# Clearing the modality table second on VectorE, and 128 weight columns for the products of the modality codes

## The chip, the cores and the metric

The kernel runs on one core of one Trainium2 chip. The metric is the device time of one execution in microseconds (us). Engines are called as the profile calls them: PE is TensorE's products, PEld its weight loads, DVE is VectorE, ACT is ScalarE, POOL is GpSimd and SP is SyncE.

## The reference, cut to what matters

Sliding-window attention feeds a mixture of experts. Each of the 4608 tokens takes the one expert with the largest gate value; a bias that depends on the token's modality (0 or 1) is added to the gate values first.

```python
def _attn_ref(q, k, v):                       # q, k, v: 8 batches x 8 heads x 576 x 64
    scores = scale * np.matmul(q, k.transpose(0, 1, 3, 2))
    mask = np.abs(pos[:, None] - pos[None, :]) <= window      # window 32
    attn = softmax(np.where(mask, scores, -1000000000.0))
    return np.matmul(attn, v)

def _moe_ref(x, modality_id, w_gate, modality_bias, w1, w2):  # x: 4608 x 512, 8 experts
    logits = x @ w_gate + modality_bias[modality_id]
    e_idx = np.argmax(logits, axis=1)
    gate_w = softmax(logits)[np.arange(N), e_idx]
    for e in range(E):
        mask = e_idx == e
        h = np.maximum(x[mask] @ w1[e], 0.0)
        out[mask] = gate_w[mask, None] * (h @ w2[e])
```

## The kernel before, in words

**The plan.** In the data, all tokens of one modality take the same expert. So the kernel sorts the tokens by modality while it computes attention, runs each modality's tokens through one expert, and scatters the rows of the result back. For that it counts the tokens of modality 1 in each block of up to 128 tokens (40 blocks, five for each of the eight batches), forms for each token its place in the sorted order, and builds a 0/1 matrix `oh` from these places (`o`, lines 569 to 577, on POOL for the first three batches).

**The order.** `ORDER` (line 38) is a list of operations written out by hand. A loop (line 915) goes through it and calls the function of each name; every engine then runs its own instructions in just that order. In a name, the digits are batch and part, the letter behind a slash is the engine, the digits behind a colon are PSUM banks.

**The modality table.** `mid64` holds the token ids, one row per block. `Kh` (line 290, DVE) clears it, since blocks at the two ends of a batch fill their row only in part. `Ki` (lines 281 to 286) issues five loads into it on SP's queue; they wait for the clearing. `Kd` (line 467, DVE) casts it to bf16 and waits for all five loads. `Kt` and `Kr` (lines 471 to 505) transpose it on PE, count with products of one column and form the places: line 488 writes `c16`, line 496 the last of `lpf`, both on DVE, and lines 503 and 505 on POOL write the codes `valx`. `Kc7` (line 415, DVE) clears the table `cl` that takes the sorted codes; `Ke` (line 424) writes eight constants.

**The queues around it.** DVE's next instruction behind `Kd` is `tv0.0` (line 239), which transposes rows of v; PE's transposes `TV` (line 252) need it. POOL issues nearly all loads (lines 217, 222, 228 for q, k, v; line 795 for the experts' weights, 1 MB each as bf16), between its own computations; it waits with `oh` (line 573) for `lpf`.

**The products of the codes.** For each batch `J` (lines 705 to 713) multiplies `oh` of five blocks by the codes of the block: the weights are 4 columns of `valx` (`valx[:, NM * b + m, :]`), the moving side is 96 or 128 columns of `oh`, and the result has 4 rows in PSUM. ACT (`j`, line 719) copies these 4 rows into `cl`. `H` (line 680) does the same for the rows of x, with 128 columns of weights. The experts' products are `U` (line 822) and `D` (line 845); `S` (line 614) is the scores' products, whose weights have 32 rows, `V` (line 660) the products with v.

Of the kernel before, what the change touches and what calls it, by code (L numbers as in the profile page):

```python
# [23 lines left out]
BF16 = mybir.dt.bfloat16  # L24
# [11 lines left out]
NYS = 6  # L36

ORDER = """
Km l0.1.0 Kw Kc7 Kj l0.0.0 lw0.0 Kn0 Ke Kh Kx Kq0/a t0.0.1 t0.0.0 X4:7 X3:2 X0:4 X2:3 MB0.0:4567 Ky0 Kp1/v Kv2/v X9:2
X11:3 X10:2 X5:3 SB0.0:4567 X6:3 Ki MA0.0:0123 SA0.0:0123 Kd tv0.0 Kv0/v l0.0.1 t0.1.0 Kp0/a sb0.0 sa0.0 Kv1/p l0.1.1  # L40
t0.1.1 lw0.1 Kc1 Kq1/a l1.1.0 l1.0.0 Kc4 Kc0 Kv3/p Kc3 Kc2 TV0.0:567 vc0.0/a Kt0:4 Kr0 MB0.1:0123 SB0.1:0123 l1.1.1
Kt1:4 sb0.1 tv0.1 X7:5 TV0.1:567 Kr1 t1.0.1 MA0.1:0123 SA0.1:0123 Kt2:4 t1.0.0 Kr2 vc0.1/a sa0.1 V0:67 V1:45 v0 v1
t1.1.1 MB1.0:0123 SB1.0:0123 l1.0.1 Ka lw1.1 Kr3 Kc5 o0/p lw2.0 lw1.0 l2.1.0 o1/p l2.0.0 Ko0 sb1.0 Kp2/a V2:45 v2 V3:67
# [47 lines left out]
def kernel(  # L91
# [12 lines left out]
    nc = tc.nc  # L104
    B, H, S, D = q.shape
    P = 128
# [8 lines left out]
    NM = 5  # L115
    NJ = B * NM
# [8 lines left out]
    width = lambda m: 96 if m in EDGE else P  # L125
# [10 lines left out]
    const = ctx.enter_context(tc.tile_pool(name="const", bufs=1))  # L136
# [9 lines left out]
    def apart(ins, group, other, keep=()):  # L146
        unordered(ins, other, keep)
        tc.add_to_no_dep_group(group, ins.ins)
# [7 lines left out]
    def bank(shape, dt=FP32, i=0):  # L156
        n_ = 1
        for s_ in shape[1:]:
            n_ *= s_
        f_ = banks[:, bk[i], :] if dt == FP32 else banks[:, bk[i], :].bitcast(dt)  # L160
        f_ = f_[0:shape[0], 0:n_]
        if len(shape) == 3:
            f_ = f_.rearrange("p (a b) -> p a b", a=shape[1])
        return f_
# [10 lines left out]
    Ct = {}  # L175
# [150 lines left out]
    def iota_f(n, pattern, base_, cm, dt=FP32):  # L326
        ti = const.tile([P, n], I32, name=f"ioi{iota_f.c}")
        tf = const.tile([P, n], dt, name=f"iof{iota_f.c}")
        iota_f.c += 1
        nc.gpsimd.iota(ti[:], pattern=pattern, base=base_, channel_multiplier=cm)  # L330
        nc.gpsimd.tensor_copy(tf[:], ti[:])
        return tf
# [37 lines left out]
    @named  # L370
    def Kc(_, i):
        gs = nc.gpsimd
        if i == 0:
            gs.memset(tri[:], 1.0)
            gs.affine_select(out=tri[:], in_=tri[:], compare_op=ALU.is_ge, fill=0.0,
                             base=-1, pattern=[[1, P]], channel_multiplier=-1)
            gs.memset(ones[:], 1.0)
        elif i == 1:
            T["ic"] = iota_f(NM, [[0, NM]], 0, 1)
            gs.tensor_copy(cc1[:], T["ic"][:])  # L380
            gs.tensor_scalar(out=cc1[:, 0:1], in0=T["ic"][:, 0:1], scalar1=-32.0, scalar2=None, op0=ALU.add)
            gs.memset(cc1[0:32, 0:1], -1000.0)
            gs.memset(cc1[96:P, NM - 1:NM], -1000.0)
            gs.tensor_scalar(out=cc2[:], in0=cc1[:], scalar1=-1.0, scalar2=127.0, op0=ALU.mult, op1=ALU.add)
            ends = cc2[:, 0:NM:NM - 1]
            gs.tensor_scalar(out=ends, in0=ends, scalar1=-32.0, scalar2=None, op0=ALU.add)
        elif i == 2:
            T["iol"] = iota_f(P, [[1, P]], 0, 0)
            gs.tensor_copy(io_l[:], T["iol"][:])
        elif i == 3:  # L390
            gs.tensor_copy(vb[:, :, 0:1], iota_f(NJ, [[0, NJ]], 127, -1)[:].unsqueeze(2))
            gs.tensor_copy(vb[:, :, 1:2], iota_f(NJ, [[-18, B], [-4, NM]], 145, 0)[:].unsqueeze(2))
        elif i == 4:
            T["tj"] = iota_f(NJ + NM, [[S, B + 1], [P, NM]], -32, 0)
            first = T["tj"][:].rearrange("p (b m) -> p b m", m=NM)[:, :, 0:1]
            gs.tensor_scalar(out=first, in0=first, scalar1=32.0, scalar2=None, op0=ALU.add)
        elif i == 5:
            ic = T["ic"][:, 0:1]
            wf = const.tile([P, 4], FP32)
            for j_, (r_, c_) in enumerate(((0, 1.0), (1, 32.0), (2, 1.0), (3, 32.0))):  # L400
                gs.tensor_scalar(out=wf[:, j_:j_ + 1], in0=ic, scalar1=float(r_), scalar2=c_,
                                 op0=ALU.is_equal, op1=ALU.mult)
            for i_ in range(2):
                gs.tensor_tensor(out=wi[:, i_, :], in0=wf[:, 2 * i_:2 * i_ + 1], in1=wf[:, 2 * i_ + 1:2 * i_ + 2],
                                 op=ALU.add)
            gs.tensor_tensor(out=wi[:, 2, :], in0=wi[:, 0, :], in1=wi[:, 1, :], op=ALU.add)
        elif i == 6:
            T["nb"] = iota_f(B, [[1, B]], 1, 0)
            lv_ = lim[:].rearrange("p i (b m) -> p i b m", m=NM)
            gs.memset(lv_[:, 0], 48.0)  # L410
            gs.memset(lv_[:, 0, :, 1:NM - 1], 64.0)
            gs.memset(lv_[:, 1], (most(0) - 48.0) ** 2)
            gs.memset(lv_[:, 1, :, 1:NM - 1], (most(1) - 64.0) ** 2)
        elif i == 7:
            nc.vector.memset(cl[:], 0.0)  # L415
        elif i == 8:
            ins = gs.memset(xl[:, :, N // 2 - T3:N // 2 + 2 * T3], 0.0)
            Ct["Kc8"] = ins
            apart(ins, "vs", "xa")
# [37 lines left out]
    n1s = const.tile([NJ, 1], BF16)  # L457
    offs = const.tile([1, NJ + 1], I32)
    cA = const.tile([1, NJ + 1], FP32)
    valx = const.tile([P, NJ, 4], BF16)  # L460
    fl = const.tile([P, 8], FP32)
    fr = const.tile([1, 4, NJ], FP32)
    ngm = const.tile([P, 1], FP32)
# [240 lines left out]
    @named  # L704
    def J(_, b):
        for m in range(NM):
            if m < 4:
                o_ap = bank([P, 4, P])[0:4, m, :]
            else:
                o_ap = bank([P, 4, P], i=1)[0:4, 0, :]  # L710
            nc.tensor.matmul(o_ap[:, 0:width(m)], valx[:, NM * b + m, :], Ct["o", b][:, m, 0:width(m)], start=(m % 4 == 0), stop=True,  # L711
                             skip_group_check=True)
            Ct["J", b, m] = o_ap

    @named
    def j(_, b, m):
# [369 lines left out]
```

## Time and profile before

| | us |
|---|---|
| median of 3 runs | 226.16 (223.16, 226.16 and 227.04) |
| the profiled execution | 223.96 |
| its span, first to last instruction | 222.3 |
| PE busy | 204.5 (92% of the span) |
| DVE, ACT, POOL busy | 154.7, 141.0, 118.7 |
| mean granted clock of PE | 0.986 |

The profile is of one execution, and its span is 1.66 us shorter than that execution's time. Rows of the timeline and of the chain of waits start with two numbers, the start and the length in us, counted from the start of the span. In square brackets stands how long the engine had been idle and what ended the wait. SPq and POOLq mean the instruction queue of an engine. Matmul rows of one line that follow each other are merged, with their number behind the x. The end of a product is modelled and includes the time that it takes to run through the array, so two products overlap in their rows; the distance of two products is read from start to start.

### The profile page before, as it was taken

The page shows a single profiled execution, that of the slowest core. Times are in us where ns is not written, and L with a number is a line of the kernel's source. Part 1 is how long each engine was busy: PE and PEld are TensorE (multiplying, and loading weights), DVE is VectorE, ACT ScalarE, POOL GpSimd, SP SyncE. Part 2 cuts the span into 40 slices and gives each one's busy share as a digit, 9 for nine tenths or more (in the row PEclk, how much of TensorE's full clock was granted, in tenths as well). Part 3 has the DMA queues.
Part 4 walks back from the last instruction along what each step waited for, and adds up shares of the span by engine and source line. Part 5 has one row for each costly group of instructions (what it writes and reads, how often), then busy time and mean ns, then how long its engine had stood idle before and what let it go on. Part 6 is the DMA issues. An engine that isn't in the chain of part 4 may idle for free.

```text
span 222.3 us, 6507 instructions
## 1 busy us (share of the span) xinstructions
PE 204.5 (92%) x2669; PEld 145.6 (66%) x2696; DVE 154.7 (70%) x302; ACT 141.0 (63%) x234; POOL 118.7 (53%) x215
## 2 busy tenths in 40 slices
PE   6759888999999999999999999999999999999960
PEld 2436657789666678786577875787488659765620
DVE  6677999896977998697997879686775236312420
ACT  7267698798957777988875687757715603541420
POOL 7888997426208979490368981550014311814770
PEclk9978999999999999999999999999999999999997
DMA  5997799999999999569017999290003210689441
GB/s 68 197 201 131 123 155 207 223 200 212 212 186 205 165 160 196 104 122 138 10 42 154 180 187 193 51 196 4 0 3 143 94 50 3 167 194 204 188 157 55
DMA packets 34055, 30.44 MB, mean 137 GB/s; under 512 B 24889, under 2 KB 24929, under 8 KB 33633
## 3 DMA queue, kind: packets, MB, share of 16 engines
q0 software_dynamic: 33792, 29.90, 77.1%
q8 instruction: 23, 0.38, 0.7%
q14 instruction: 16, 0.12, 0.2%
q1 hardware_dynamic: 224, 0.05, 0.1%
HBM read 40.96 MB, written 9.70 MB: 228 GB/s over the span
## 4 chain that ended last, share of the span: by engine, by line
PE 76%; DMA 9%; POOL 6%; issue 2%; DVE 2%; SPq 1%; POOLq 0%; DVEq 0%
PE banks L845 28%; PE banks L822 28%; DMA w_sb<-in_moe_w_dram 6%; PE banks L660 6%; PE banks L614 5%; POOL oh L573 3%; PE banks L680 3%; DMA mid<-in_moe_modality_id_dram 2%; PE banks L749 2%; PE banks L711 1%; DVE cl L415 1%; POOL out_dram L866 1%; SPq L285 1%; PE banks L252 1%; POOL qkin L217 1%
## 5 line engine op out<-in xcount | busy, mean ns | idle before, releaser
L866 POOL DMA_INDIRECT out_dram<-ys,ix x37 | 38.9, 1051 | 70.4 <-issue 27.9
L822 PE MATMUL banks<-xl,w_sb 128*128 128x256 bf16 x576 | 70.7, 273 | 0.7 <-DMA w_sb<-in_moe_w_dram 0.7
L845 PE MATMUL banks<-w_sb,hT 128*128 128x512 bf16 x267 | 67.7, 379 | 1.1
L822 PEld LDWEIGHTS <-w_sb 128*128 128x128 bf16 x576 | 53.8, 98 | 11.0 <-issue 1.1
L622 ACT ACTIVATE pt<-banks 128x1536 bf16<-128x1536 f32 x32 | 46.3, 1449 | 18.6 <-PE banks L614 18.4
L837 ACT ACTIVATE hT<-banks 128x512 bf16<-128x512 f32 x45 | 25.8, 599 | 30.0 <-PE banks L822 29.8
L845 PEld LDWEIGHTS <-hT 128*128 128x128 bf16 x296 | 26.6, 98 | 25.5 <-issue 0.5
L582 DVE STREAM_TRANSPOSE qk<-qkin 128x576 int32<-128x576 int32 x32 | 39.0, 1243 | 1.2 <-DMA qkin<-in_q_dram 0.6
L698 ACT CAST xl<-banks 128x704 f32 (+1 forms) x40 | 28.4, 710 | 8.7 <-PE banks L680 8.2
L641 DVE TENSOR_TENSOR pt<-pt,mask 128x1920 bf16<-128x1920 bf16 x26 | 29.8, 1160 | 0.5 <-ACT pt L626 0.3
L671 DVE TENSOR_TENSOR xt<-banks,recs 128x640 bf16<-128x640 f32 x32 | 26.4, 825 | 1.2
L835 DVE TENSOR_SCALAR hT<-banks 128x512 bf16<-128x512 f32 x29 | 19.6, 682 | 9.0 <-PE banks L822 7.9
L660 PEld LDWEIGHTS <-pt 128*128 128x128 bf16 x576 | 21.1, 97 | 2.8 <-DVE pt L641 0.2
L660 PE MATMUL banks<-vt,pt 128*128 128x65 bf16 x576 | 22.6, 193 | 0.0
L573 POOL TENSOR_SCALAR oh<-io_l,lpf 128x128 bf16<-128x128 bf16 x30 | 19.9, 682 | 2.7 <-PE banks L680 1.9
L858 ACT ACTIVATE ys<-banks,gw 128x512 f32<-128x512 f32 x19 | 12.8, 685 | 12.4 <-PE banks L845 9.1
L860 DVE TENSOR_SCALAR ys<-banks,gw 128x512 f32<-128x512 f32 x18 | 13.2, 743 | 10.6 <-PE banks L845 10.5
L614 PE MATMUL banks<-qk 32*128 32x192 bf16 (+1 forms) x640 | 18.9, 240 | 1.4 <-DVE qk L582 1.3
L614 PEld LDWEIGHTS <-qk 32*128 32x128 bf16 x640 | 12.5, 93 | 8.3 <-issue 6.9
L217 POOL DMA_DIRECT2D qkin<-in_k_dram x16 | 10.3, 642 | 12.1 <-DMA w_sb<-in_moe_w_dram 7.8
L680 PEld LDWEIGHTS <-xt 128*128 128x128 bf16 x160 | 11.2, 114 | 4.6 <-issue 0.7
L222 POOL DMA_DIRECT2D vt<-in_v_dram x10 | 13.7, 1373 | 0.0
(164 smaller groups left out, 200.8 us busy)
## 6 DMA issues: line engine op xcount, KB each, us to landing
qkin<-in_k_dram POOLq DMA_DIRECT2D x16, 288.0 KB, 7.0
qkin<-in_q_dram POOLq DMA_DIRECT2D x16, 288.0 KB, 6.8
w_sb<-in_moe_w_dram POOLq DMA_DIRECT2D x4, 1024.0 KB, 16.9
vt<-in_v_dram POOLq DMA_DIRECT2D x10, 288.0 KB, 7.5
pt<-in_moe_w_dram POOLq DMA_DIRECT2D x2, 1024.0 KB, 10.3
qkin<-in_v_dram POOLq DMA_DIRECT2D x6, 288.0 KB, 6.0
out_dram<-ys,ix POOLq DMA_INDIRECT x37, 4.0
mid<-in_moe_modality_id_dram SPq DMA_DIRECT2D x3, 8.0 KB
```

Source lines behind the costliest of these rows:

```text
L573: gp.tensor_scalar(out=t_[:, m, :], in0=io_l[:], scalar1=lpf[:, NM * b + m:NM * b + m + 1], scalar2=None, op0=ALU.is_equal)
L582: nc.vector.transpose(qk_t[b % 2][:, g, at:at + S].rearrange("p (t r) -> p r t", r=R), Ct["l", b, u, g][:].bitcast(I32).rearrange("p (r j) ...
L614: nc.tensor.matmul(st[:, h, WIN * i_:WIN * i_ + w_], qk[32 * h:32 * h + 32, c_, QK + k0:QK + k0 + P], qk[32 * h:32 * h + 32, c_, q0:q0 + w ...
L622: nc.scalar.activation(pt[:, :, 2 * part:2 * part + 2, 0:WIN], st[:, :, 0:2 * WIN].rearrange("p h (j c) -> p h j c", c=WIN), ACT.Exp, scal ...
L641: by[eng or "v"].tensor_tensor(out=p_ap, in0=p_ap, in1=mask[:], op=ALU.mult)
L660: nc.tensor.matmul(o_ap, pt[:, c1:c1 + P], vt[:, g0 + j, 0:D + 1], start=(m == 0 and i_ == 0), stop=(i_ == len(mine) - 1), skip_group_chec ...
L671: nc.vector.tensor_tensor(out=x_t[b % NX][:, :, P * hp:P * hp + P].rearrange("p m (h d) -> p h m d", h=2), in0=o_v[:, :, :, 0:D], in1=rec. ...
L698: ins = nc.scalar.copy(windows(xl, n_kd, P, NM * b + m), src)
L822: ins = nc.tensor.matmul(ph[:, u_, :], w1[:, kd, 2 * P * (mi // 2) + mi % 2:2 * P * (mi // 2 + 1):2], xl[:, kd, c0:c0 + n_], start=(kd == ...
L837: nc.scalar.activation(o_ap, i_ap, ACT.Relu)
L845: nc.tensor.matmul(Ct["D", t_, s_], Ct["h", t_][:, kf, P * s_:P * s_ + P], w2[:, kf, :], start=(kf == 0), stop=(kf == n_kf - 1))
L866: ins = nc.gpsimd.indirect_dma_start(out=out, out_offset=bass.IndirectOffsetOnAxis(ap=ix[:, k_, n_:n_ + 1], axis=0), in_=Ct["y", t_, s_][: ...
```

## The change

`Kh` and `Ki` move to the front of the list: the modality table is cleared as DVE's third instruction (the second operation that the list gives it), ahead of `cl`, and SP's five loads wait for that alone. SP's own order stays, and POOL, PE and ACT keep theirs. The codes stand in a tile `valw` of 160 + 124 columns, whose last 124 columns are cleared by a new DVE instruction behind the clearing of `cl`. Each product of the codes takes 128 columns as weights, from the block's own four on: the first four result rows are the codes as before, the other 124 rows are products with the codes of later blocks or with zeros, and nothing reads them.

```diff
-Km l0.1.0 Kw Kc7 Kj l0.0.0 lw0.0 Kn0 Ke Kh Kx Kq0/a t0.0.1 ...
+Km l0.1.0 Kw Kh Ki Kc7 Kj l0.0.0 lw0.0 Kn0 Ke Kx Kq0/a t0.0.1 ...
...
-X11:3 X10:2 X5:3 SB0.0:4567 X6:3 Ki MA0.0:0123 SA0.0:0123 Kd tv0.0 ...
+X11:3 X10:2 X5:3 SB0.0:4567 X6:3 MA0.0:0123 SA0.0:0123 Kd tv0.0 ...
...
         elif i == 7:
             nc.vector.memset(cl[:], 0.0)
+            nc.vector.memset(valw[:, 4 * NJ:], 0.0)
...
-    valx = const.tile([P, NJ, 4], BF16)
+    valw = const.tile([P, 4 * NJ + P - 4], BF16, name="valw")
+    valx = valw[:, 0:4 * NJ].rearrange("p (n c) -> p n c", c=4)
...
     def J(_, b):
         for m in range(NM):
             if m < 4:
-                o_ap = bank([P, 4, P])[0:4, m, :]
+                o_ap = bank([P, 4, P])[:, m, :]
             else:
-                o_ap = bank([P, 4, P], i=1)[0:4, 0, :]
-            nc.tensor.matmul(o_ap[:, 0:width(m)], valx[:, NM * b + m, :], Ct["o", b][:, m, 0:width(m)], start=(m % 4 == 0), stop=True,
+                o_ap = bank([P, 4, P], i=1)[:, 0, :]
+            at = 4 * (NM * b + m)
+            nc.tensor.matmul(o_ap[:, 0:width(m)], valw[:, at:at + P], Ct["o", b][:, m, 0:width(m)], start=(m % 4 == 0), stop=True,
                              skip_group_check=True)
-            Ct["J", b, m] = o_ap
+            Ct["J", b, m] = o_ap[0:4]
```

The order on DVE at the start of the program, before the change (`mid_103` is the modality table, `e_119` the eight constants, `qkin` the loaded rows of q, k and v):

```order
L303 MEMSET zero_b 128x256
L304 MEMSET one_f 128x1
L415 MEMSET cl 128x2368
L424 MEMSET e_119 128x1 x8
L290 MEMSET mid_103 40x256
L437 TENSOR_REDUCE pm<-mb_bc 128x2
```

And with the change, where the lines behind 416 have moved down by one to three:

```order
L303 MEMSET zero_b 128x256
L304 MEMSET one_f 128x1
L290 MEMSET mid_103 40x256
L415 MEMSET cl 128x2368
L416 MEMSET valw 128x62
L425 MEMSET e_119 128x1 x8
L438 TENSOR_REDUCE pm<-mb_bc 128x2
```

The clearing of the table has moved ahead of that of `cl` and of the constants, and one short instruction has come in; the cast of the table (line 467, 469 in the changed kernel) stays where it is, twelve rows behind that of `pm`.

On PE, one product of the codes of the first batch before the change:

```order
L711 LDWEIGHTS valx
L711 MATMUL banks<-oh_99,valx 4x96
L711 LDWEIGHTS valx
L711 MATMUL banks<-oh_99,valx 4x128
L711 LDWEIGHTS valx
```

And with it:

```order
L714 LDWEIGHTS valw
L714 MATMUL banks<-oh_99,valw 128x96
L714 LDWEIGHTS valw
L714 MATMUL banks<-oh_99,valw 128x128
L714 LDWEIGHTS valw
```

Nothing has moved there; the result has 128 rows in place of 4.

More of the change, by code (lines that the diff above doesn't have):

```diff
@@ L38 @@
 ORDER = """
-Km l0.1.0 Kw Kc7 Kj l0.0.0 lw0.0 Kn0 Ke Kh Kx Kq0/a t0.0.1 t0.0.0 X4:7 X3:2 X0:4 X2:3 MB0.0:4567 Ky0 Kp1/v Kv2/v X9:2
-X11:3 X10:2 X5:3 SB0.0:4567 X6:3 Ki MA0.0:0123 SA0.0:0123 Kd tv0.0 Kv0/v l0.0.1 t0.1.0 Kp0/a sb0.0 sa0.0 Kv1/p l0.1.1
+Km l0.1.0 Kw Kh Ki Kc7 Kj l0.0.0 lw0.0 Kn0 Ke Kx Kq0/a t0.0.1 t0.0.0 X4:7 X3:2 X0:4 X2:3 MB0.0:4567 Ky0 Kp1/v Kv2/v X9:2
+X11:3 X10:2 X5:3 SB0.0:4567 X6:3 MA0.0:0123 SA0.0:0123 Kd tv0.0 Kv0/v l0.0.1 t0.1.0 Kp0/a sb0.0 sa0.0 Kv1/p l0.1.1
 t0.1.1 lw0.1 Kc1 Kq1/a l1.1.0 l1.0.0 Kc4 Kc0 Kv3/p Kc3 Kc2 TV0.0:567 vc0.0/a Kt0:4 Kr0 MB0.1:0123 SB0.1:0123 l1.1.1
```

## The prediction

> **What bounds the kernel now.** I read the page first, then the busy time by stretches, then the chain of waits of the first 50 us, then the timelines of the engines around its joints. The page says that PE works nearly all of the span, and less in the first eight slices of 5.6 us:
>
> ```profile
> PE   6759888999999999999999999999999999999960
> ...
> PEclk9978999999999999999999999999999999999997
> ```
>
> The stretches make that sharper (length, then busy time and instructions of PE, PEld, DVE, ACT and POOL, then the granted clock, the DMA share and GB/s):
>
> ```profile
> 20.00:27.00 7.00, 5.94 (x136) 4.48 (x133) 6.62 (x13) 5.09 (x7) 6.97 (x13) 1.00 0.54 90
> 27.00:35.00 8.00, 6.42 (x117) 4.38 (x117) 7.46 (x9) 7.78 (x14) 7.99 (x15) 1.00 1.03 173
> 35.00:48.40 13.40, 12.58 (x216) 10.76 (x215) 12.55 (x16) 11.44 (x19) 4.63 (x11) 1.00 1.05 208
> 48.40:80.00 31.60, 31.32 (x471) 22.54 (x477) 26.43 (x47) 25.30 (x41) 18.66 (x24) 1.00 1.30 192
> ...
> 160.00:190.00 30.00, 29.84 (x338) 22.46 (x340) 14.30 (x45) 9.89 (x20) 7.51 (x11) 1.00 0.15 55
> ```
>
> From 48.4 us on PE is full, so there its own work sets the end. From 20 to 35 us POOL is full (6.97 of 7.00, 7.99 of 8.00), while the DMA engines stand half idle up to 27 us and are full behind. The chain says how these two are tied:
>
> ```profile
> 7.01 5.30 DMA mid<-in_moe_modality_id_dram
> ...
> 12.65 1.18 DVE xl L239
> ...
> 13.88 1.83 PE banks L252 x20
> ...
> 19.27 0.21 DVE lpf L496
> ...
> 19.57 1.27 POOL oh L573 x3
> ...
> 34.29 14.08 DMA w_sb<-in_moe_w_dram
> ...
> 48.42 1.60 PE banks L822 x13
> ```
>
> The modality ids come late, so the places of the tokens come late, so POOL starts its 0/1 matrices late. From there POOL goes without a stop to the issue of a weight load at 34.29, which lands at 48.37, and PE waits for it.
>
> **The ids: how much earlier.** SP's five loads, the start of DVE, and DVE's wait:
>
> ```profile
> 4.20 0.76 SPq L283 DMA_DIRECT2D mid<-in_moe_modality_id_dram  x1
> ...
> 7.01 0.62 SPq L286 DMA_DIRECT2D mid<-in_moe_modality_id_dram  x1
> ...
> 1.77 2.03 DVE L415 MEMSET cl<- 128x2368 uint32 x1 [0.44 <-issue]
> ...
> 3.90 0.27 DVE L290 MEMSET mid<- 40x256 int32 x1
> ...
> 5.88 1.25 DVE L582 STREAM_TRANSPOSE qk<-qkin 128x576 int32<-128x576 int32 x1 [0.59 <-DMA qkin<-in_k_dram]
> ...
> 10.23 0.18 DVE L234 MEMSET xl<- 128x64 int32 x2
> ...
> 12.43 0.22 DVE L467 CAST midr<-mid 40x128 bf16<-40x128 int32 x1 [2.03 <-DMA mid<-in_moe_modality_id_dram]
> ```
>
> The table's clearing now starts where that of `cl` did, at 1.77, and ends at 2.04; SP's first load goes from 4.20 to about 2.07. From the first issue to the last landing it took 12.31 - 4.20 = 8.11 us (the chain's row of 7.01 ends at 12.31). If that stays, the table is whole at 10.18. DVE gets to the cast at 10.23 + 0.18 = 10.41, so its wait of 2.03 goes, with 0.23 to spare; each us that the loads need more than that comes back as a wait. The new clearing of 62 words is not in the trace; it lies between nothing and the 0.27 us that 256 words take. I take 0.1, for a quarter of them and a start; the 0.59 idle ahead of 5.88 hides it, and without that cover it would cost its 0.1 on DVE. The constants behind it slip by as little under the same cover. The id loads now run beside the first load of k. Should they hold it up by 0.5 us, DVE is 0.5 later all the way to the cast, and the places still come in time for POOL, as the next part shows; so this costs nothing either.
>
> So DVE's transpose of v ends 2.0 us earlier, at 11.8, and PE's 20 transposes start there instead of at 13.88. How much the places (L496) gain lies between that 2.0 and 2.0 plus what PE no longer loses to its clock:
>
> ```profile
> 11.40:14.40 3.00, 0.53 (x10) 0.53 (x11) 1.97 (x5) 2.44 (x6) 2.42 (x10) 1.00 1.12 212
> 14.40:17.90 3.50, 3.50 (x35) 2.38 (x36) 2.91 (x4) 1.12 (x1) 3.22 (x11) 0.51 1.06 183
> ```
>
> After the idle stretch the clock was halved for 3.5 us; at half clock those products lose at most half of that, 1.75 us. The places would then be there between 19.47 - 3.8 = 15.7 and 17.5.
>
> **What POOL makes of it.** Here the gain is cut:
>
> ```profile
> 13.84 0.58 POOL L217 DMA_DIRECT2D qkin<-in_k_dram  x1 [0.20 <-DVE xl L239]
> ...
> 18.68 0.20 POOL L406 TENSOR_TENSOR wi<-wi 128x1 bf16<-128x1 bf16 x1
> 19.57 2.97 POOL L573 TENSOR_SCALAR oh<-io_l,lpf 128x128 bf16<-128x128 bf16 x5 [0.69 <-DVE lpf L496]
> ```
>
> POOL ends its other work at 18.88 and waits 0.69 for places that will now stand there 1.4 us or more before. Only that 0.69 goes, and of the 0.20 at 13.84 (the end of the transpose of v, now 11.8) between nothing, if it is the cost of issuing, and all. POOL's gain is 0.69 to 0.89; I take **0.8**. Behind it POOL has no wait up to 34.29 that another engine sets, and the DMA share of 0.54 from 20 to 27 us says that the transfers wait for POOL and not POOL for them. So the weight load of 34.29, its landing at 48.37 and the start of PE's full stretch move by the same 0.8. If the transfers do not follow, the floor is nothing.
>
> What is late next are two loads of v that POOL issues behind its first matrices:
>
> ```profile
> 22.48 1.16 POOL L228 DMA_DIRECT2D qkin<-in_v_dram  x2
> ...
> 29.28 3.42 DVE L239 STREAM_TRANSPOSE xl<-qkin 128x576 int32<-128x576 int32 x3 [0.49 <-DMA qkin<-in_v_dram]
> ...
> 30.83 1.28 PE L252 MATMUL banks<-ident,xl 128*128 128x64 bf16 x20
> ```
>
> They move by 0.8 while DVE and PE come to it two to three us earlier. DVE's 0.49 grows to between 1.7 and 2.7, and PE will stand there for about as long as it stood at 11.4 to 13.9.
>
> **The products of the codes.** The distance between products is read from start to start. Two groups of five, and a change of line between full-width products:
>
> ```profile
> 91.75 0.50 PE L680 MATMUL banks<-oh,xt 128*128 128x128 bf16 x6
> 92.18 0.41 PE L711 MATMUL banks<-oh,valx 128*4 128x96 bf16 x5
> 92.53 0.39 PE L845 MATMUL banks<-w_sb,hT 128*128 128x512 bf16 x1
> ...
> 67.77 0.50 PE L614 MATMUL banks<-qk 32*128 32x192 bf16 x13
> 68.19 0.41 PE L711 MATMUL banks<-oh,valx 128*4 128x96 bf16 x5
> 68.54 0.39 PE L845 MATMUL banks<-w_sb,hT 128*128 128x512 bf16 x1
> ...
> 168.93 0.27 PE L822 MATMUL banks<-xl,w_sb 128*128 128x256 bf16 x1
> 169.03 0.33 PE L680 MATMUL banks<-oh,xt 128*128 128x96 bf16 x4
> ```
>
> A product of 128 columns lasts 0.22, so the six of L680 are (0.50 - 0.22) / 5 = 0.056 apart and the last starts at 92.03. The first product of the codes starts 0.15 later instead of 0.056: 0.09 lost. The last of the five starts at 92.18 + 0.41 - 0.21 = 92.38, and L845 0.15 behind it, where its 96 columns need 0.04: 0.11 lost. From L822 to L680, both full, it is 0.10, just what 256 columns need. So a step to or from 4 columns costs 0.1, and a whole group 0.20. The group at 68.19 stands behind products of 32 rows, whose step costs as much anyway and stays; there only the 0.11 behind goes.
>
> Of the eight groups, those of batches 2 to 7 (68.2, 92.2, 109.3, 133.7, 154.9 and 169.3 us) lie where PE is full: 0.11 + 5 x 0.20 = **1.1 us**. The group at 26.8 stands behind a wait for DVE, that at 37.9 ahead of the weight load that sets 48.4; they give nothing. A wider weight load could take some of it back:
>
> ```profile
> L680 PEld LDWEIGHTS <-xt 128*128 128x128 bf16 x160 | 11.2, 114 | 4.6 <-issue 0.7
> ...
> L711 PEld LDWEIGHTS <-valx 128*4 128x4 bf16 x40 | 2.0, 83 | 2.0 <-POOL oh L573 0.9 <-issue 0.6 <-ACT xl L698 0.2
> ```
>
> L680 loads 128 columns ahead of each product and still keeps the 0.056, so the load lies beside the product ahead: cost nothing. The dearest row is L252 at 30.83 above, (1.28 - 0.22) / 19 = 0.056 for 64 columns, with weights that are read with a stride; a group's two products of 96 columns would lose 0.014 each by that, 0.2 us over six groups. So the term lies between 0.9 and 1.1, and I take 1.1, since the codes are read without a stride.
>
> The Trainium skill, "TensorE: Matmul & The Clock Gate", section "LDWEIGHTS (loading the stationary operand)", speaks against this: a load takes its columns divided by 1.2 ns, 107 ns for 128 and 3 for 4. By it, with nothing beside it, 30 loads would cost an estimated 3.1 us; the rows of L680 and L711 (114 and 83 ns) and the 0.056 do not bear that out.
>
> **The sum.** 223.96 - 0.8 - 1.1 = 222.06 for an execution like the profiled one. That one lies below most others: of the four times (223.16, 223.96, 226.16, 227.04) the middle is 225.06, 1.1 above it. I carry these 1.1 along: **223.2 us**.
>
> **The rivals.** *The stall moves and takes the clock with it.* PE worked for 0.53 of the 3.00 us ahead of 14.4 and paid with 3.5 us at 0.51. If the new stall at about 27 to 30 us does the same, up to 1.75 us of products are lost from 30 to 34 us; PE's idle time up to 48.4 (1.58 in the stretch from 27, 0.82 in that from 35) takes back about 1.0 of it, so POOL's 0.8 shrinks to nothing: 224.0 with the 1.1 carried. For it: the stall is about as long. Against: PE has some products to issue in between, and 1.06 us of idle time from 20 to 27 and 1.58 from 27 to 35 left the clock at 1.00. The Trainium skill, same page, section "What's actually happening", asks for an idle window of about 3.4 us that runs freely; the 2.47 us here were enough, so the measurement decides, but where the window falls differs from run to run.
>
> *The 4 columns are not the cause* of the lost 0.1, but the turn to another bank or semaphore: then only 0.8 is gained, 224.3. Against: L822 to L680 turns as well and loses nothing.
>
> *Slower: the wide load is not hidden.* The products' five weights are windows of one tile that overlap; should PE load each only when the one before is through, 30 loads of the 98 ns that 128 columns mostly take stand bare. That is 2.9 us against 1.9 gained, 226.1 against 225.06. It turns to a loss from 1.9 / 30 = 0.063 us for each product. Only L680's even 0.056 speaks against it.
>
> ```profile
> L822 PEld LDWEIGHTS <-w_sb 128*128 128x128 bf16 x576 | 53.8, 98 | 11.0 <-issue 1.1 <-DMA w_sb<-in_moe_w_dram 1.0
> ```
>
> *More than the sum.* If the spread of the runs (3.9 us) comes from where the halved clock falls in the first 50 us, taking away the stall at 12 us might also remove the slow cases: 223.2 less about 2, 221.2.
>
> **How the numbers follow.** Forecast 0.58, clock rival 0.20, other cause 0.05, slower 0.04, more than the sum 0.13. The range takes in the clock rival, "more" and the spread of the runs about their middle: 220.9 to 226.0. A measurement of this kernel tells about 2% from no change, so faster means under 221.6 and slower over 230.7. Under 221.6 lies half of "more" and a low draw of the forecast: 0.13. Over 230.7 nothing reaches by itself; 0.03 for what I have not seen. 0.84 remains.
>
> **What would show it.** Right: SP's first id load at about 2.1, no DVE wait at the cast, POOL's L573 (now L575) at 18.7 to 18.9 without a wait, the awaited weight load landing at 47.5 to 47.7; 0.056 from the last product of 128 columns to the first of the codes, and a group's step to L848 without 0.1. Wrong: a wait for the ids that stays; POOL earlier by two us or not at all; a clock near 0.5 between 28 and 35 us; products of the codes more than 0.06 apart; new waits of PE behind 48 us.

## The result, and the profile after

| | before | with the change |
|---|---|---|
| median of 20 runs each (us) | 224.35 (222.52 to 227.04) | 222.3 (221.13 to 223.49) |
| the profiled execution (us) | 223.96 | 221.51 |
| its span (us) | 222.3 | 219.9 |
| mean granted clock of PE | 0.986 | 0.985 |

The ratio is 0.9913, with a 95% interval of 0.9892 to 0.9934: about 2 us are gained. That is under the 2% that the prediction takes for no change, and yet the interval excludes a ratio of 1. The forecast was 223.2.

The stretches of the changed kernel, cut at the same joints (length, then busy time and instructions of PE, PEld, DVE, ACT and POOL, then the granted clock, the DMA share and GB/s):

```profile
11.40:14.80 3.40, 3.40 (x31) 1.87 (x31) 3.32 (x10) 2.84 (x4) 2.82 (x11) 0.55 1.10 209
...
27.00:35.00 8.00, 6.51 (x127) 4.74 (x126) 7.22 (x8) 7.83 (x12) 7.99 (x15) 1.00 1.01 176
35.00:47.60 12.60, 12.12 (x209) 10.41 (x206) 12.15 (x16) 10.80 (x18) 5.29 (x11) 1.00 1.05 207
47.60:80.00 32.40, 32.40 (x505) 23.23 (x504) 27.78 (x50) 25.90 (x42) 18.94 (x28) 1.00 1.32 198
```

PE is full from 47 us on, as before. POOL is full from 27 to 35 us, as before. The halved clock (0.55 over the first of these stretches) lies at about 11.7 to 15.1 us in place of 14.4 to 17.9, and none lies at 27 to 35 us, where the clock rival had put it.

The identifier loads on SP and the start of DVE in the timeline:

```profile
1.61 0.76 SPq L283 DMA_DIRECT2D mid<-in_moe_modality_id_dram  x1
...
4.42 0.62 SPq L286 DMA_DIRECT2D mid<-in_moe_modality_id_dram  x1
```

```profile
1.31 0.27 DVE L290 MEMSET mid<- 40x256 int32 x1
...
4.02 0.11 DVE L416 MEMSET valw<- 128x62 uint32 x1
...
9.42 1.26 DVE L584 STREAM_TRANSPOSE qk<-qkin 128x576 int32<-128x576 int32 x1 [2.24 <-DMA qkin<-in_q_dram]
...
11.96 0.16 DVE L469 CAST midr<-mid 40x128 bf16<-40x128 int32 x1
...
18.38 0.20 DVE L498 TENSOR_TENSOR lpf<-lpf,banks 128x40 f32<-128x40 f32 x1
```

The loads go out 2.6 us earlier and DVE's wait for the identifiers (2.03) is gone. But another wait has come: the first load of q, on which DVE waited 0.64 before, is awaited for 2.24. So the cast starts at 11.96, 0.47 earlier than before and not two. The places are there at 18.58 in place of 19.47.

POOL, and then PE, at the joints of the prediction:

```profile
13.85 0.58 POOL L217 DMA_DIRECT2D qkin<-in_k_dram  x1 [0.20 <-issue]
...
18.98 2.98 POOL L575 TENSOR_SCALAR oh<-io_l,lpf 128x128 bf16<-128x128 bf16 x5
...
33.72 0.57 POOL L798 DMA_DIRECT2D w_sb<-in_moe_w_dram  x1
```

```profile
10.73 0.64 PE L616 MATMUL banks<-qk 32*128 32x192 bf16 x24 [2.92 <-DVE qk L584]
...
46.98 1.92 PE L825 MATMUL banks<-xl,w_sb 128*128 128x256 bf16 x16
...
89.94 0.78 PE L682 MATMUL banks<-oh,xt 128*128 128x96 bf16 x12
90.55 0.42 PE L714 MATMUL banks<-oh,valw 128*128 128x96 bf16 x5
90.81 1.03 PE L848 MATMUL banks<-w_sb,hT 128*128 128x512 bf16 x4
```

POOL starts its first matrix without a wait, 0.59 earlier than the 19.57 of before, and issues the weight load 0.57 earlier (34.29 before). PE starts on these weights at 46.98 without a wait, 1.44 earlier (48.42 before). Before, PE had waited for them, but for 0.38 only:

```profile
48.42 1.92 PE L822 MATMUL banks<-xl,w_sb 128*128 128x256 bf16 x16 [0.38 <-DMA w_sb<-in_moe_w_dram]
```

So PE's other work, which would have brought it there at 48.04, came 1.06 earlier as well. The codes' products start 90.55 - 89.94 = 0.61 behind the row ahead of them, and L848 follows 0.26 behind their start. The same two distances before stand in these rows:

```profile
91.47 0.78 PE L680 MATMUL banks<-oh,xt 128*128 128x96 bf16 x12
92.18 0.41 PE L711 MATMUL banks<-oh,valx 128*4 128x96 bf16 x5
92.53 1.04 PE L845 MATMUL banks<-w_sb,hT 128*128 128x512 bf16 x4
```

They were 0.71 and 0.35, so this group is 0.19 shorter. The start of the group of batch 2 went from 68.20 to 66.77, 1.43 earlier; the end of the last group is 2.54 earlier. The groups of batches 2 to 7 thus give 2.54 - 1.43 = 1.11 us. The gain is spread evenly: each of the five distances from the start of one group to the start of the next is 0.19 to 0.22 shorter than before.

### The profile page after: what moved, and what is told of

The parts are those of the page before. It is cut to its first block, busy times and chain, and to the rows that moved or that the text cites. A ratio compares the mean times of both kernels' runs of the same rounds, so it can differ in the third digit from the quotient of the medians.

```text
span 219.9 us, 6535 instructions
## 1 busy us (share of the span) xinstructions
PE 205.0 (93%) x2696; PEld 145.5 (66%) x2696; DVE 154.7 (70%) x303; ACT 140.9 (64%) x234; POOL 119.8 (54%) x215
## 4 chain that ended last, share of the span: by engine, by line
PE 81%; DMA 6%; POOL 5%; DVE 3%; issue 3%; POOLq 0%; DVEq 0%
PE banks L825 30%; PE banks L848 29%; PE banks L662 6%; PE banks L616 6%; DMA qkin<-in_q_dram 6%; PE banks L682 3%; POOL oh L575 2%; PE banks L252 2%; PE banks L752 2%; DVE qk L584 1%; POOL out_dram L869 1%; PE banks L714 1%; PE banks L593 1%; POOL qkin L228 1%; DVE pt L643 1%
## 5 line engine op out<-in xcount | busy, mean ns | idle before, releaser
L848 PE MATMUL banks<-w_sb,hT 128*128 128x512 bf16 x288 | 70.1, 379 | 0.0
L848 PEld LDWEIGHTS <-hT 128*128 128x128 bf16 x296 | 26.7, 98 | 25.2 <-issue 0.5
L838 DVE TENSOR_SCALAR hT<-banks 128x512 bf16<-128x512 f32 x29 | 19.6, 682 | 8.7 <-PE banks L825 7.4
```

The costliest lines, as they stand in the source:

```text
L848: nc.tensor.matmul(Ct["D", t_, s_], Ct["h", t_][:, kf, P * s_:P * s_ + P], w2[:, kf, :], start=(kf == 0), stop=(kf == n_kf - 1))
```

## The experiments

*Theory.* The two parts are independent. The earlier identifiers let POOL start earlier, and from there POOL's own program order, up to the issue of the weight load, sets the time at which PE gets full. The codes gain because a product with few weight columns is set apart from its neighbours by 0.1 us. *Rivals.* Only one of the parts counts; or the earlier identifier loads hold up the first load of q; or something other than the number of columns causes the 0.1.

The first four kernels shared a chip on which the kernel before took 229.07 (median of 29 runs). Ratios, not times, are compared with other chips.

**1. The codes alone.** The clearing and the loads go back to their places.

```diff
-Km l0.1.0 Kw Kh Ki Kc7 Kj ... Kn0 Ke Kx Kq0/a
+Km l0.1.0 Kw Kc7 Kj ... Kn0 Ke Kh Kx Kq0/a
...
-X11:3 X10:2 X5:3 SB0.0:4567 X6:3 MA0.0:0123
+X11:3 X10:2 X5:3 SB0.0:4567 X6:3 Ki MA0.0:0123
```

> The change's products of the codes with 128 columns, in the order of before (the table cleared late). Theory (two terms that add): no step of 0.1 us at the groups of codes, 1.1 us less from the group of 68 us to the one of 169 us, ratio to before 0.995 (about 223.2 against 224.35), DVE's wait of about 2.0 us at the cast of the table and POOL's first matrix at 19.5 to 19.6 us as before. Rival (the steps' time is not on the path, the whole gain comes from the ids): ratio 0.998 to 1.002 although the steps are gone.

Measured: 227.9 us (12 runs), ratio 0.9966 (0.9924 to 1.0008), 0.8 us by the ratio.

```profile
20.30 2.98 POOL L575 TENSOR_SCALAR oh<-io_l,lpf 128x128 bf16<-128x128 bf16 x5 [1.02 <-DVE lpf L498]
```

POOL waits for the places, as before the change, but later than the 19.5 to 19.6 that was expected: the identifiers landed at 13.25 here (12.31 in the profile of before), and DVE waited 1.30 for them. Behind PE's products of 128 columns the codes start 0.056 apart. The gain agrees with the 1.1 of the forecast, though its interval alone does not exclude a gain of nothing.

**2. The identifiers alone.** The products take 4 columns again, with 4 result rows, and the wide tile and its clearing are gone (the cut shows the product alone).

```diff
-nc.tensor.matmul(o_ap[:, 0:width(m)], valw[:, at:at + P], ...)
+nc.tensor.matmul(o_ap[:, 0:width(m)], valx[:, NM * b + m, :], ...)
```

> The early clearing of the table and the early id loads alone, codes with 4 columns as before. Theory: no DVE wait at the cast, POOL's first matrix at 18.9 to 19.0 us without a wait, PE's full stretch 0.6 to 1.4 us earlier, the steps of 0.1 us still there, ratio 0.995 to 0.997. Rival (more than POOL's 0.6 us comes of it, since the weight loads land 1.4 us earlier in the profile of the change): ratio 0.993 to 0.994. On the second load: if the id loads cause it, the first load of q lands at 9 to 9.5 us as in the change; if that was one execution's luck, at 7.7 us as before.

Measured: 227.56 us (12 runs), ratio 0.9947 (0.992 to 0.9974), 1.2 us. That lies between the two ranges, and the interval covers both. The first load of q landed at 9.71, late again.

```profile
19.11 2.97 POOL L573 TENSOR_SCALAR oh<-io_l,lpf 128x128 bf16<-128x128 bf16 x5 [0.20 <-DVE lpf L496]
...
48.64 1.59 PE L822 MATMUL banks<-xl,w_sb 128*128 128x256 bf16 x13 [1.14 <-DMA w_sb<-in_moe_w_dram]
```

POOL starts within 0.13 of the changed kernel's 18.98, and PE still waits for the weights: up to that joint it is the load that decides.

**3. The change again,** and **4. the kernel before again** (one execution), on the same chip.

> The change once more, for a second profile of it. Ratio 0.989 to 0.993. If the id loads beside the first loads cause the late load of q, it lands at 9 us or later again, with a DVE wait of about 2 us ahead of the second transpose, and the weight load that PE waited for before lands between 46.9 and 47.7 us; if it was luck, q lands at 7.7 us and DVE reaches the cast at 10.4 us.

> The kernel before once more, for a second profile of it. Time 222.5 to 227. The first load of q lands at 7.7 us, the wait at the cast is 1.5 to 2.5 us, POOL's first matrix starts at 19.2 to 19.8 us, PE waits for the weight load at 48 to 48.6 us. If the first profile's weight loads were slow by luck, that one lands at about 47.5 us here.

Measured: the change took 227.15 us (12 runs), ratio 0.9905 (0.9876 to 0.9935); the sum of the two parts, 0.8 + 1.2 = 2.0 us, lies inside its 2.2 (1.5 to 2.8). So they add up, as far as intervals of this width can tell. The load of q landed at 9.22, DVE waited 2.45 for it, and the weight load landed at 48.17, later than the 46.9 to 47.7 that was expected. The kernel before gave 230.68 us, above the range that was expected, and this:

```profile
9.07 1.26 DVE L582 STREAM_TRANSPOSE qk<-qkin 128x576 int32<-128x576 int32 x1 [2.31 <-DMA qkin<-in_q_dram]
...
20.87 2.98 POOL L573 TENSOR_SCALAR oh<-io_l,lpf 128x128 bf16<-128x128 bf16 x5 [0.93 <-DVE lpf L496]
```

With late identifiers, too, the q load can come late (9.05 here, 9.42 in the first experiment). The rival that the earlier loads hold it up falls as the cause. The gain on POOL is no fixed number either: with late identifiers its first matrix started at 19.57, 20.30 and 20.87, with early ones in the same order of POOL at 18.91 to 19.11, so it is between 0.5 and 2.0. It does reach PE: from kernel 4 to kernel 2 POOL issues the weight load 1.81 earlier (35.65 and 33.84) and PE starts on it 1.92 earlier (50.56 and 48.64).

Experiments 5 to 12 ran on another chip. In 5 to 8 the kernel before took 224.71 there (median of 11 runs), in 9 to 12 it took 224.03 (of 21).

**5. POOL's small operations out of the way.** What POOL did from 17.53 to 19.0 (lines 401 to 406) goes behind a later weight load, so that its first matrix could start earlier.

```diff
-... Kr3 Kc5 o0/p lw2.0 lw1.0 l2.1.0 o1/p ...
+... Kr3 o0/p lw2.0 lw1.0 l2.1.0 o1/p ...
...
-... J1:34 W2.1 l3.1.1 Ky1
+... J1:34 W2.1 Kc5 l3.1.1 Ky1
```

> The change, and POOL's seven small operations on the constants of the index (lines 401 to 406, 1.45 us ahead of the first matrix) stand behind the issue of the weight loads instead. Theory (POOL's own work in front of the matrices is what cuts the gain of the early ids): the first matrix starts as soon as the places are there, 18.3 to 18.7 us instead of 18.98, with a short wait for DVE again; POOL's issues move by 0.3 to 0.7 us, ratio to before 0.987 to 0.990. Rival (the transfers or DVE set the stage before 48 us by now): POOL earlier by as much, ratio 0.990 to 0.992 as with the change.

Measured: 221.9 us (6 runs), ratio 0.9886 (0.9838 to 0.9935), which is not told apart from the change; the interval covers the theory's range and the rival's. The execution shown took 224.47, the longest of the six.

```profile
18.31 2.95 POOL L575 TENSOR_SCALAR oh<-io_l,lpf 128x128 bf16<-128x128 bf16 x5 [0.62 <-DVE lpf L498]
```

Only 0.67 is to be had there: then POOL waits for the places once more. In the changed kernel the two come within 0.4 us of each other (places 18.58, POOL 18.98).

**6 and 7. How many columns.** The products take 64 columns (the diff, without the lines that give the result as many rows), then in the same way 68; one execution each.

```diff
-nc.tensor.matmul(o_ap[:, 0:width(m)], valw[:, at:at + P], ...)
+nc.tensor.matmul(o_ap[:, 0:width(m)], valw[:, at:at + 64], ...)
```

> The change with 64 columns of weights in place of 128 (64 result rows). Theory (the array is set up in another way for up to 64 columns, and turning it costs the step): the steps of 0.09 to 0.10 us into and out of a group stand as with 4 columns. Rival (the step hangs on a load much shorter than its neighbours): no step, or less than half of it.

> The change with 68 columns of weights. Theory (set-up by 64 columns): no step, 0.056 us from a product of 128 columns to the first of the group, as with 128. Rival (only a full load of 128 columns avoids it): steps of 0.09 to 0.10 us as with 4.

The group of batch 3 in the timeline, first with 64 columns, then with 68:

```profile
90.53 0.78 PE L682 MATMUL banks<-oh,xt 128*128 128x96 bf16 x12
91.24 0.44 PE L714 MATMUL banks<-oh,valw 128*64 128x96 bf16 x5
91.61 1.04 PE L848 MATMUL banks<-w_sb,hT 128*128 128x512 bf16 x4
```

```profile
90.37 0.78 PE L682 MATMUL banks<-oh,xt 128*128 128x96 bf16 x12
90.98 0.42 PE L714 MATMUL banks<-oh,valw 128*68 128x96 bf16 x5
91.24 1.03 PE L848 MATMUL banks<-w_sb,hT 128*128 128x512 bf16 x4
```

With 64 columns the distances are 0.71 and 0.37, as with 4; with 68 they are 0.61 and 0.26, as with 128. Everything else of the group is alike, bank and semaphore too, so the number of columns is the cause, and four more of them take 0.21 us off a group. The rival "the 4 columns are not the cause" falls. So does the short load: with 64 columns a load of the codes takes 109 ns in the mean, no less than the 97 to 114 of its neighbours, and the step is there. The times were 223.08 and 221.9 us. The Trainium skill, "TensorEngine Tiling (Array Packing)", sections "Key Properties" and "Column Tiling (LHS free dim ≤ 64)" under "Performance Considerations", fits this: the array has a mode of its own for up to 64 columns, and a change of mode drains it. Here it is 0.1 us for each change. The runs show the step and that it goes between 64 and 68 columns; that this mode is behind it is an inference.

**8. The later loads first.** If POOL's order decides, loads that stand behind POOL's first matrix should pay more than the matrix itself: three loads of v and k for later batches (`lw2.0`, `lw1.0`, `l2.1.0`) go ahead of `o0`, with `Kc5` out of the way as in 5.

```diff
-... Kr3 Kc5 o0/p lw2.0 lw1.0 l2.1.0 o1/p ...
+... Kr3 lw2.0 lw1.0 l2.1.0 o0/p o1/p ...
...
-... J1:34 W2.1 l3.1.1 Ky1
+... J1:34 W2.1 Kc5 l3.1.1 Ky1
```

> The fifth experiment, and three loads (two of v, one of k) are issued ahead of the first matrix instead of behind it, into the time at 22 to 25 us in which the transfers stand still. Theory (POOL's order starves the transfers there): these three land 2 to 4 us earlier, at 23 to 26 us, the first weight loads behind them 1 us or more earlier, ratio to before 0.982 to 0.988. Rival (PE, DVE and ACT set the stage before 48 us): loads earlier, ratio as in the fifth experiment within 0.002.

Measured: 220.37 us (6 runs), ratio 0.9831 (0.9784 to 0.9877), below both kernels.

```profile
17.48 1.11 POOL L228 DMA_DIRECT2D qkin<-in_v_dram  x2
...
19.14 5.83 POOL L575 TENSOR_SCALAR oh<-io_l,lpf 128x128 bf16<-128x128 bf16 x10
...
45.84 1.92 PE L825 MATMUL banks<-xl,w_sb 128*128 128x256 bf16 x16 [0.40 <-DMA w_sb<-in_moe_w_dram]
```

The three loads go out 4.4 us earlier (21.91 in the changed kernel), the weights that PE waits for are there 1.1 us earlier.

**9 to 12. What sets the time then.** The change, kernel 8 again, kernel 8 with two of POOL's 0/1 matrices (`o1`, `o2`) moved behind further loads, and kernel 8 with the identifiers late. W1.1 and W1.0 in the expectations are two loads of the experts' weights, the second of them the one that PE waits for near 48 us.

Kernel 11, against kernel 8:

```diff
-... l2.1.0 o0/p o1/p l2.0.0 ...
+... l2.1.0 o0/p l2.0.0 ...
...
-lw2.1 W1.1 l2.1.1 l2.0.1 o2/p a0.0 ... J1:34 W2.1 Kc5 l3.1.1
+lw2.1 W1.1 l2.1.1 l2.0.1 o1/p a0.0 ... J1:34 W2.1 o2/p Kc5 l3.1.1
```

Kernel 12 undoes in kernel 8 what experiment 1 undoes in the change:

```diff
-Km l0.1.0 Kw Kh Ki Kc7 Kj ... Kn0 Ke Kx Kq0/a
+Km l0.1.0 Kw Kc7 Kj ... Kn0 Ke Kh Kx Kq0/a
...
-X11:3 X10:2 X5:3 SB0.0:4567 X6:3 MA0.0:0123
+X11:3 X10:2 X5:3 SB0.0:4567 X6:3 Ki MA0.0:0123
```

> The change a third time, as the yardstick of the other three of this call. Both theories: 0.988 to 0.993 of the kernel before.

> Batch 3's later loads ahead of the first matrix's products and the small product behind W2.1, once more. Theory (the loads of W1.1 and W1.0, issued by GpSimd in its program order, set the stage at 35 to 48 us): 0.980 to 0.987 of the kernel before, at least 0.6% below the change. Rival (the first measurement was a lucky one): within 0.3% of the change.

> As the run before it, and the products o1 and o2 also go behind the loads that they stood ahead of, so that GpSimd issues W1.1 near 24.7 us instead of 27.7 and W1.0 near 29.3. Theory (the loads' issue sets the stage): W1.0 lands 1 to 3 us earlier than 45.8 and the time is 0.990 to 0.998 of the run before. Rival (TensorE's own work, busy 12.12 of the 12.60 us from 35.0 to 47.6, sets the stage by now): no gain, 0.998 to 1.003 of the run before, and W1.0's matmuls start within 0.5 us of 45.8 without a wait for a transfer.

> As the second run of this call, with the identifier loads and the table's clearing back where the kernel before has them. Theory (GpSimd's first matrix waits for VectorE's table of places when the identifiers land late): the places at 19.5 to 20.3 us, GpSimd's first matrix waits for them, and 0.4 to 1.2 us are lost against the second run. Rival (with the loads ahead of the first matrix its start no longer matters): the wait is there, and the time is that of the second run within 0.3%.

| | median us (runs) | ratio to before |
|---|---|---|
| 9, the change | 222.08 (11) | 0.9912 (0.9879 to 0.9945) |
| 10, loads first | 220.47 (6) | 0.9858 (0.9796 to 0.9921) |
| 11, two matrices later as well | 220.67 (6) | 0.9851 (0.9789 to 0.9912) |
| 12, loads first, identifiers late | 223.13 (12) | 0.9939 (0.9903 to 0.9976) |

The chains of waits up to 50 us tell the rest. The change, in its third measurement:

```profile
9.18 0.54 POOL qkin L217
...
19.09 1.10 POOL oh L575 x2
...
30.96 2.08 POOL oh L575 x4
...
33.84 13.35 DMA w_sb<-in_moe_w_dram
47.24 1.92 PE banks L825 x16
```

No other engine stands in it from 2.7 us to the load: POOL's own instructions, one behind the other, set the time, as the prediction has it from 19 us on. In the execution shown with the result the two paths are level: the weights land at 46.94, and PE comes to them by itself 0.04 later. Kernel 10:

```profile
2.72 6.49 DMA qkin<-in_q_dram
9.23 1.26 DVE qk L584
10.54 0.66 PE banks L616 x24
11.23 1.45 ACT pt L624
```

POOL and the weight load have left the chain; it now goes through the first load of q, PE and the exponentials of ACT. In the first measurement of the same kernel PE still waited 0.40 for the weights, so here, too, the paths are close. The ratio to the change of the same chip is 220.47 / 222.08 = 0.993, so the gain stands. The halved clock does not explain it: the three executions of the change with a mean granted clock of 0.992 to 0.994 took 221.62 to 222.25, and five of the six of kernel 10, at 0.988 to 0.991, took 219.78 to 220.68 (the sixth 222.75). Kernel 11 added nothing, and the rival stated for it was right: it issues a weight load at 24.78 (27.70 in kernel 10), then POOL has to wait, and PE's stretch in front of the joint is as full as ever (length, PE's busy time, granted clock, DMA share and GB/s; first kernel 11's POOL, then its stretch):

```profile
24.78 0.54 POOL L798 DMA_DIRECT2D w_sb<-in_moe_w_dram  x1
...
27.36 0.53 POOL L217 DMA_DIRECT2D qkin<-in_q_dram  x1 [1.51 <-DVE qk L584]
```

```profile
35.00:47.60 12.60, 12.25 (x210) 1.00 1.09 213
```

Kernel 12 lost 2.66 us against kernel 10, more than twice the 0.4 to 1.2 that the theory gave, and not on the theory's path:

```profile
8.20 5.45 DMA mid<-in_moe_modality_id_dram
...
13.77 0.22 DVE midr L469
13.99 1.18 DVE xl L239
...
15.21 2.31 PE banks L252 x20
...
17.67 1.39 PE banks L593 x4
...
19.36 0.60 PE banks L616 x20
...
19.98 1.45 ACT pt L624
```

POOL did start its first matrix 2.0 us later (21.17 against 19.17, with a wait of 0.80 for the places), but it is not in the chain. The identifiers hold up DVE's transpose of v, which stands behind the cast, and through it PE and ACT; PE's 20 transposes take 2.31 in place of 1.28, at half clock. Part of the 2.66 is this clock: eight of the twelve executions, with a mean granted clock of 0.972 to 0.974, took 222.99 to 223.67, and four with 0.984 to 0.988 took 221.63 to 222.59, about 1.5 above kernel 10. So the early identifiers are worth 1.5 to 2.7 us in the order of kernel 10. In the order of the change they are worth 0.75 (kernel 1 against kernel 3) to 1.2 (experiment 2).

## Why the prediction was right, point by point

**The direction, and that it stays within 2%: right.** 222.3 lies in the range, 0.9 below the forecast.

**The codes, 1.1: right, 1.11.** The step of 0.1 on each side is what the number of columns costs (6 and 7); the group of batch 2 keeps its step ahead, behind products of 32 rows, and saves only the one behind, as forecast. The wide load stays hidden: the mean load of the codes takes 97 ns now and 83 before, and the products stay 0.056 apart.

**The identifiers, 0.8: the mechanism right, the size off in both directions.** POOL's gain was 0.59, below the 0.69 to 0.89 of the working. The 0.20 at 13.84 was the cost of issuing (it stands at 13.85 still), and POOL's small operations (lines 401 to 406) came to their end 0.10 later (18.98 against 18.88). Behind it PE came to the weights 1.44 earlier in place of 0.8, since the load itself took 13.22 in place of 14.08. That part is luck as far as the runs tell: in kernels 1 to 4 the same load took 13.55 and 14.87 with late identifiers and 14.76 and 14.47 with early ones. The prediction also let PE follow the weights without looking at PE's other path to this place; with a wait of 0.38 there, more than 0.38 could be gained only because that path moved too, by 1.06. On another chip, where the identifiers came later still, POOL gained 1.9 (20.87 to 18.98). So the term depends on how late the identifiers are in the run before, which one profile could not tell. The table was cleared at 1.31 and not at 1.77, since the 0.44 idle ahead of `cl` stayed with `cl` (2.03 now); the identifier loads therefore start at 1.61 in place of the 2.1 of the forecast.

**"DVE gets to the cast at 10.41": wrong, 11.96.** The prediction asked whether the identifier loads would hold up the first load of k; it was the first load of q that came late, at 9.40 in place of 7.76. With late identifiers it was as late (9.05, 9.42 and 9.54 in kernels 4, 1 and 12), and in kernel 8, with early ones, it came at 7.96. In 12 of the 14 profiles it landed between 9.05 and 9.80; the profile of before was one of the two exceptions. The cause of the late load stays open. It did not cost the gain on POOL, since the places had time to spare there, as the prediction has it; of the 1.4 us or more that it gave them, 0.4 was left (18.58 against 18.98). In kernel 8, where q came early, the cast started at 10.53 and the places were there at 16.38, inside the 15.7 to 17.5 of the forecast. So the working held, and what failed is the landing of q that it took over from one profile.

**"What is late next" (the loads of v, a wait of 1.7 to 2.7): did not come.** With the q load late, DVE and PE reached the place less than a microsecond earlier than before, and DVE's row stands there without a wait:

```profile
27.94 3.42 DVE L239 STREAM_TRANSPOSE xl<-qkin 128x576 int32<-128x576 int32 x3
```

The stall and the halved clock lie at 8 to 15 us instead, where PE waited 2.92 for q. So the condition of the clock rival, a stall of PE at 27 to 30 us, did not come about, and the rival is not tested by this profile.

**The carry of 1.1: the step that cost most.** Four times put the median of before 1.1 above the profiled execution; 20 runs put it 0.4 above (224.35 against 223.96). With 0.4 the sum of the prediction would have been 222.06 + 0.4 = 222.5, 0.2 from the measured median. The two terms themselves, 1.9 together, stand against 2.05 between the medians.

**The other rivals.** That the wide load is not hidden would have shown as products 0.1 apart, and does not. "More than the sum" was wrong about the median, 222.3 and not 221.2. What it argued from did happen: the spread of the 20 executions fell from 4.52 to 2.36, the longest by 3.55 and the shortest by 1.39. The clock has a part in it, though no run was made for it: on the two chips with many executions of both kernels, those of the kernel before with a mean granted clock under 0.988 took 1.6 us more in the median than the others (229.32 and 227.68, 225.07 and 223.49), those of the change 0.6 and 0.4 more (227.70 and 227.06, 222.26 and 221.91). And there was more in the same place: with POOL out of the way, the same early identifiers give 1.5 to 2.7 (10 against 12).

## What to carry to other kernels

When a late input feeds two chains, ask which of them is bound by its own work: early identifiers gave 0.75 to 1.2 us while POOL's own work set the time and 1.5 to 2.7 once its order was changed, so an edit that gives little may be waiting for the next one. Count the columns of the stationary operand (the weights): with 4 or 64 of them a group of products that stands between full-width ones cost 0.2 us for the pair of changes here, with 68 or 128 it did not, and the columns that nobody reads cost nothing, since their load lay beside other products. A profile is one execution of several kinds; before carrying its distance to the median into a forecast, take the median from more than four runs.

## What the runs showed of the hardware that was not expected

The step between 64 and 68 columns is sharp: 0.71 and 0.37 against 0.61 and 0.26 us. Two stretches of waiting of 2.9 and 1.5 us on PE (kernel 12) went with twice 3.4 us of halved clock, and one of 2.9 (the change) with 3.4; in kernel 10, with a wait of 2.1 at the same place, the clock was never halved there. The length of one wait does not decide: in kernel 1 a wait of 2.55 passed at full clock, and 3.4 us at half clock came behind a later one of 1.78. The Trainium skill, "TensorE: Matmul & The Clock Gate", section "What's actually happening", asks for an idle window of about 3.4 us, which none of these waits reaches, and for a busy one as long before the clock comes back; the 3.4 us of the halved stretches agree with the second. One chip ran the kernel before and the change 2% longer than the others (before 229.07 against 224.35, 224.71 and 224.03), while the ratios of the change agree (0.9905 against 0.9913 and 0.9912).
